# The last half pair in two quarters of queries, with four output blocks left behind the loop

## The chip, the cores and the metric

The kernel runs on one core of a Trainium2 chip. The metric is the device time of one execution in microseconds. Engines in this text: TensorE (PE, its weight loads PEld), VectorE (DVE), ScalarE (ACT), GpSimd (POOL) and SyncE (SP), which here only issues DMAs.

## The reference

```python
# x: 2048 rows (S) of 512 (D); 32 heads of 16
g = sigmoid((x * gate_w).sum(-1, keepdims=True))
q, k, v = heads of x @ wqkv
a = (softmax(q @ k.T / 4) @ v, heads side by side) @ wo
b = Re(DFT over the rows of the DFT over the columns of x)   # as products with four given matrices
return g * a + (1 - g) * b
```

All arrays are float32. The softmax runs over all 2048 keys for each of the 2048 queries and 32 heads.

## The kernel before

Rows come in 16 blocks of 128 (`NB`), heads in 16 pairs (`NP`). Large products run in the format float32r with each operand split into a rounded part and a rest; three products of the parts (rounded x rounded, rounded x rest, rest x rounded) make one full product. `halves_of` (L201) issues such a product as two 64-row matmuls that run side by side on the array, one into each bank of a two-bank PSUM tile. One call of it is a "pair" in this text.

The main loop (L1217) has 512 steps: 16 pairs of heads, for each two halves of 1024 queries (h), for each 16 blocks of keys (kb). A step computes the scores of two heads, 128 keys and 1024 queries (`qk`, two times 512 queries, c = 0 and 1: the first into the two-bank tile "wide1", the second into single banks), their exponentials on ScalarE, and the values (`pv`): four matmuls, for c and the head j, each into 17 rows (16 of values, one of sums) of one PSUM bank `pvb`, summed over the 16 key blocks. Values are taken two steps at a time, in even steps, one or two steps behind the scores. After a half, `quotients` copies pvb to SBUF and gathers the sums, and `divide` some steps later divides and stores the rows in DRAM, from where they are loaded again as operands.

Step numbers: pair p begins at step 32 p. From step 285 (MIX) on, each step takes one piece of other TensorE work, the fill (`next(fill)`), from a generator `outputs`. In an even step the fill stands ahead of that step's scores, in an odd step behind them. So the queue of TensorE reads: odd step's scores, odd step's fill, even step's fill, even step's scores, values of two steps, next odd step's scores.

From step 461 on the fill is the output projection. `mix_heads(t, steps)` makes output block t from the first 12 pairs of heads in nine pairs of matmuls, spread over as many steps as `steps` has numbers, (4, 5) being four pairs in the first step and five in the second, and (2, 2, 2, 3) for blocks 0, 2 and 4. `mix_some(t, (0, 1))` adds pairs 12 to 15 of the heads to the blocks t and t + 4: part 0 and part 1, three pairs each; for t of 8 to 11 there is a part 2, which is the last half pair (pair 15, second 1024 queries). Each of these takes its two banks from `pair_banks()`, the tile "wide0" of a pool with one buffer, and ends with `take_in`, two instructions on VectorE that read the two banks, weigh them with g and add them to the rows y. `store_out` sends finished rows out on SP's queue.

The fill at the end of the loop is: blocks 0 to 15 by `mix_heads` (steps 461 to 498), `mix_some` for 8, 9, 10, then 0, 1, 2 (499 to 510), one empty piece. Behind the loop (from L1284) the last half pair's values are copied, turned by TensorE so that the sums lie beside them, divided, turned back and rounded; then come the parts that are left: block 3's (with 7), all of 11's (with 15), and part 2 of 8, 9, 10 and 11 (with 12 to 15).

Of the kernel before, what the change touches and what calls it, by code (L numbers as in the profile page):

```python
# [52 lines left out]
HALVED = MIX + NB * (LATER - CROSS)  # L53
SLOW = 3
EVERY = 24
# [13 lines left out]
def build(tc, xT, xr, wqkv, wo, wrT, wiT, cr, ci, ct, gate, out):  # L69
    nc = tc.nc  # L70
    with ExitStack() as ctx:
# [152 lines left out]
        def qk(p, h, kb, c, pss):  # L224
# [3 lines left out]
            for j in range(2):  # L228
                b = 64 * j
                nc.tensor.matmul(pss[j], ks[b:b + 50, kb * P:(kb + 1) * P],  # L230
                                 qs[b:b + 50, q0:q0 + 512], start=True, stop=True)

        psk, order_ = [], ["d0", "d1", "k0"]

# [538 lines left out]
        with ExitStack() as pa:  # L773
# [21 lines left out]

            def pv(p, h, kb, es):
                for c, j, r in quads:
                    nc.tensor.matmul(pvb[r:r + VC, :], va[:, kb, 2 * p + j, :], es[c][j],  # L798
                                     start=kb == 0, stop=kb == NB - 1, tile_position=(0, r))

# [13 lines left out]
            def divide(p, h, ob, lc):  # L814
# [19 lines left out]
                store(1, ol)  # L834


            ys, oc = {}, {}
# [314 lines left out]

            def mix_some(t, parts):

                ps = pair_banks()
                ps = ps[:, 0, :], ps[:, 1, :]
                for k in parts:
                    mix_rest(t, ps, k, k == parts[0], k == parts[-1])
                    if k == parts[0]:
                        yield  # L1160
# [4 lines left out]
                yield  # L1165

            def outputs():

                for t in range(NB - LATER, NB - CROSS):
                    yield from spectral(t)  # L1170
                yield from crosses()
                for c in range(NC):
                    for t in range(4 * c, 4 * c + 4):
                        yield from mix_heads(t, (2, 2, 2, 3) if t < 2 * SLOW and t % 2 == 0 else (4, 5))
                    if c < 2:
                        output_rows(c + 2)
                for t in (8, 9, 10):
                    yield from mix_some(t, (0, 1))
                for t in range(3):
                    yield from mix_some(t, (0, 1))  # L1180
                yield

            groups = {}

            def part(t, *ks):

                if t not in groups:
                    if t in (3, 9):
                        ps = pair_banks()
                        groups[t] = ps[:, 0, :], ps[:, 1, :]  # L1190
                    else:
                        groups[t] = bank2() if t == 8 else (bank(), pvb if t == 11 else bank())
                for k in ks:
                    mix_rest(t, groups[t], k, k == 0 or 7 < t < 11, k == (2 if t > 3 else 1))

            now = [0]
            fill, operands = outputs(), output_operands()
            halves, halved, pend = [], [], []

# [17 lines left out]
            for step in range(NP * PERIODS):  # L1217
# [42 lines left out]
                if done and done[2] == NB - 1:  # L1260
                    halved.append((step + (10 if done[0] < NP - 2 else 7 if done[0] < NP - 1 else 3), quotients(*done[:2])))
                if halved and halved[0][0] <= step:
# [4 lines left out]
                    if p_ == NP - 2 + (h_ == 0):  # L1267
                        output_last(h_)
                pend.append((p, h, kb, es))
                sum_quarters(step)  # L1270
# [9 lines left out]

            halves_ = [slice(0, 256), slice(256, 512)]
            blocks_ = [slice(s * P, (s + 1) * P) for s in range(4)]
            ob = ap.tile([P, 512], F32, tag="ob", name="ob", bufs=2)
            oh, ol = (cw.tile([P, 512], F32R, tag=tag, name=tag) for tag in ("chi", "clo"))  # L1284
            direct[1].append((oh, ol))
            for c, copy in zip(halves_, (nc.vector.tensor_copy, nc.scalar.copy)):
                copy(ob[:, c], pvb[:, c])
            part(3, 1)
            turned, spread = bank(), bank()
            for q in blocks_:  # L1290
                nc.tensor.transpose(turned[:, q], ob[:, q], ident)  # L1291
            rl = sm.tile([P, 16], F32, tag="lc", name="lc")
            nc.vector.reciprocal(rl.rearrange("p (s n) -> p s n", n=4),
                                 turned.rearrange("p (s n m) -> p s n m", n=4, m=32)[:, :, :, DH])
            for i, c in enumerate(halves_):
                heads = [v.rearrange("p (n m) -> p n m", m=32) for v in (rb[:, c], turned[:, c])]
                nc.vector.tensor_mul(heads[0], heads[1],  # L1297
                                     rl[:, 8 * i:8 * i + 8].rearrange("p (n m) -> p n m", m=1).to_broadcast([P, 8, 32]))
            for q in blocks_:
                nc.tensor.transpose(spread[:, q], rb[:, q], ident)  # L1300
            part(11, 0, 1)

            def scaled(t, j):

                o = ap.tile([P, D], F32, tag="take", name="take", bufs=3)
                nc.scalar.mul(o, groups[t][j], g[:, t + 4 * j:t + 4 * j + 1])
                nc.gpsimd.tensor_add(ys[t + 4 * j], ys[t + 4 * j], o)

            scaled(3, 0)
            for c in halves_:  # L1310
                nc.scalar.copy(oh[:, c], spread[:, c])
            for c in halves_:
                nc.vector.tensor_sub(ol[:, c], spread[:, c], oh[:, c].bitcast(F32))
            scaled(3, 1)
            store_out(3)
            for t in (8, 9, 10, 11):
                part(t, 2)
            for j in range(2):
                scaled(9, j)
            for t in (8, 10, 11):  # L1320
                for j in range(2):
                    take_in(t + 4 * j, groups[t][j])
            for j, queue in enumerate((nc.sync, nc.scalar)):
                for t in (8, 10, 9, 11):
                    queue.dma_start(out[(t + 4 * j) * P:(t + 4 * j + 1) * P, :], ys[t + 4 * j])

# [26 lines left out]
```

## Time and profile before

| what | value |
|---|---|
| three runs | 1700.26, 1700.48, 1703.22 us, median 1700.48 |
| the profiled execution | 1700.53 us, span 1698.7 us |
| granted TensorE clock | 0.999 |
| matmuls busy (TensorE) | 99% of the span |
| ScalarE busy | 90% |
| VectorE busy | 68% |
| GpSimd busy | 46% |

The span runs from the first to the last instruction of the profiled execution. [...] In the chain of waits each piece is the work that the next piece had to wait for. In a line of the timeline, what stands in brackets is the time in which the engine was idle ahead of the instruction and what ended it.

### The profile page before, as it was taken

The page shows a single profiled execution, that of the slowest core. Times are in us where ns is not written, and L with a number is a line of the kernel's source. Part 1 is how long each engine was busy: PE and PEld are TensorE (multiplying, and loading weights), DVE is VectorE, ACT ScalarE, POOL GpSimd, SP SyncE. Part 2 cuts the span into 40 slices and gives each one's busy share as a digit, 9 for nine tenths or more (in the row PEclk, how much of TensorE's full clock was granted, in tenths as well). Part 3 has the DMA queues.
Part 4 walks back from the last instruction along what each step waited for, and adds up shares of the span by engine and source line. Part 5 has one row for each costly group of instructions (what it writes and reads, how often), then busy time and mean ns, then how long its engine had stood idle before and what let it go on. Part 6 is the DMA issues. An engine that isn't in the chain of part 4 may idle for free.

```text
span 1698.7 us, 34689 instructions
## 1 busy us (share of the span) xinstructions
PE 1684.6 (99%) x13524; PEld 1039.9 (61%) x13524; DVE 1147.9 (68%) x1563; ACT 1527.5 (90%) x2545; POOL 774.5 (46%) x958
## 2 busy tenths in 40 slices
PE   9999999999999999999999999999999999999998
PEld 7798999899899783343333333334555555555554
DVE  6689889899999986666666666666113456554343
ACT  6698889888888889999999999999888888888876
POOL 5446476655554842453453445444223333434222
PEclk9999999999999999999999999999999999999999
DMA  8793566544446665645544444534416456576833
GB/s 310 266 311 77 164 196 194 157 132 126 132 125 181 188 114 108 182 109 125 149 117 120 114 122 115 118 103 104 93 55 145 149 142 147 142 175 151 197 91 127
DMA packets 150516, 249.51 MB, mean 147 GB/s; under 512 B 49696, under 2 KB 60432, under 8 KB 142992
## 3 DMA queue, kind: packets, MB, share of 16 engines
q1 hardware_dynamic: 135088, 225.92, 49.3%
q0 software_dynamic: 14688, 20.33, 5.1%
q8 instruction: 106, 1.74, 0.5%
q10 hardware_dynamic: 576, 1.05, 0.2%
q14 instruction: 58, 0.48, 0.1%
HBM read 165.94 MB, written 81.01 MB: 145 GB/s over the span
## 4 chain that ended last, share of the span: by engine, by line
PE 65%; DVE 1%; issue 0%; DVEq 0%; ACT 0%
PE pvb L798 29%; PE s L230 19%; PE s L205 10%; PE s L155 4%; PE xy L205 2%; PE s L176 1%; DVE y L913 0%; DVE mx L181 0%; DVE c L404 0%; DVE b L318 0%; PE s L1300 0%; DVEq L1349 0%; PE s L1291 0%; ACT s L179 0%; DVE rb L1297 0%
## 5 line engine op out<-in xcount | busy, mean ns | idle before, releaser
L254 ACT ACTIVATE eb<-s 128x1024 f32<-128x1024 f32 x512 | 576.9, 1127 | 65.3 <-PE s L230 65.2
L262 ACT ACTIVATE e<-s 128x512 f32<-128x512 f32 x1022 | 607.4, 706 | 0.0
L181 DVE TENSOR_REDUCE mx<-s 128x1 f32<-128x512 f32 x740 | 490.9, 688 | 48.7 <-PE s L176 38.0
L798 PE MATMUL pvb<-eb,va 128*17 128x512 f32 x2052 | 511.5, 597 | 0.0
L798 PE MATMUL pvb<-e,va 128*17 128x512 f32 x2044 | 510.7, 597 | 0.0
L179 ACT ACTIVATE s<-s 128x512 f32<-128x512 f32 x740 | 424.1, 586 | 71.9 <-PE s L176 44.4
L157 DVE TENSOR_REDUCE mx<-s 128x2 f32<-128x1024 f32 x284 | 348.1, 1226 | 172.3 <-PE s L155 172.2
L230 PEld LDWEIGHTS s<-qs,ks 50*128 50x128 f32 x2048 | 214.0, 184 | 349.6 <-ACT eb L254 242.4
L230 PE MATMUL s<-qs,ks 50*128 50x512 f32 x2048 | 417.2, 434 | 0.0
L205 PE MATMUL xy<-b,c 64*128 64x512 f32 x2280 | 377.9, 391 | 1.3 <-POOL b L374 1.3
L176 PE MATMUL s<-ks,qs 64*128 64x512 f32 x1480 | 369.3, 397 | 3.2 <-issue 1.7
L205 PEld LDWEIGHTS xy<-b,c 64*128 64x128 f32 x2280 | 276.5, 184 | 20.4 <-POOL b L374 2.0
L176 PEld LDWEIGHTS s<-ks,qs 64*128 64x128 f32 x1480 | 203.3, 184 | 35.0 <-DVE mx L181 7.7
L798 PEld LDWEIGHTS pvb<-eb,va 128*17 128x17 f32 x2052 | 71.3, 96 | 192.0 <-issue 183.3
L817 POOL DMA_DIRECT2D r_d<-lc x31 | 18.0, 580 | 267.6 <-DVE lc L816 219.4
L205 PE MATMUL s<-b,b 64*128 64x512 f32 x1050 | 136.1, 390 | 0.0
L205 PE MATMUL xy<-w,b 64*128 64x512 f32 x768 | 120.2, 391 | 0.0
L810 POOL DMA_DIRECT2D lc<-ob x124 | 63.1, 516 | 124.3 <-DVE ob L807 114.1
L155 PE MATMUL s<-ks,qs 48*128 48x512 f32 x568 | 114.7, 394 | 0.0
L205 PEld LDWEIGHTS s<-b,b 64*128 64x128 f32 x1050 | 99.5, 185 | 23.9 <-issue 1.0
L819 POOL DMA_DIRECT2D rb<-r_d x124 | 60.5, 495 | 99.0 <-DMA r_d<-lc 96.1
L405 POOL TENSOR_TENSOR c<-craw,c 128x512 fp32r<-128x512 f32 x76 | 98.2, 1292 | 14.8 <-DVE c L404 6.2
(143 smaller groups left out, 1571.1 us busy)
## 6 DMA issues: line engine op xcount, KB each, us to landing
qs<-q_d SPq DMA_DIRECT2D x92, 256.0 KB
craw<-cr SPq DMA_DIRECT2D x60, 256.0 KB
ks<-kf_d SPq DMA_DIRECT2D x48, 256.0 KB
craw<-ct SPq DMA_DIRECT2D x48, 256.0 KB
ks<-k_d SPq DMA_DIRECT2D x44, 256.0 KB
kept_None<-sum SPq DMA_DIRECT2D x40, 256.0 KB
craw<-kept_None SPq DMA_DIRECT2D x40, 256.0 KB
craw<-ci SPq DMA_DIRECT2D x32, 256.0 KB
```

The costliest lines, as they stand in the source:

```text
L155: nc.tensor.matmul(ps[:, j, :], qs[b:b + 48, qb * P:(qb + 1) * P], ks[b:b + 48, c * 512:(c + 1) * 512], start=True, stop=True)
L157: nc.vector.tensor_reduce(mx[p][:, :, qb, c], ps, axis=AX.X, op=ALU.max)
L176: nc.tensor.matmul(ps, qs[b:b + 64, qb * P:(qb + 1) * P], ks[b:b + 64, c * 512:(c + 1) * 512], start=first, stop=True, skip_group_check=True)
L179: nc.scalar.activation(ps, ps, AF.Relu)
L181: nc.vector.tensor_reduce(mx[p][:, j, qb, c // 2:c // 2 + 1], ps, axis=AX.X, op=ALU.max)
L205: nc.tensor.matmul(ps[j], lhs[r], rhs[r], start=first, stop=last)
L230: nc.tensor.matmul(pss[j], ks[b:b + 50, kb * P:(kb + 1) * P], qs[b:b + 50, q0:q0 + 512], start=True, stop=True)
L254: nc.scalar.activation(e, ps, AF.Exp, scale=SCALE)
L262: nc.scalar.activation(e[j], pss[j], AF.Exp, scale=SCALE)
L405: sub(lo, raw, hi.bitcast(F32))
L798: nc.tensor.matmul(pvb[r:r + VC, :], va[:, kb, 2 * p + j, :], es[c][j], start=kb == 0, stop=kb == NB - 1, tile_position=(0, r))
L810: nc.gpsimd.dma_start(lc[32 * n:32 * n + 32, :], ob[r + DH:r + VC, :].rearrange("p (s e) -> p s e", e=16))
```

## The change

For the second half of pair 15 only, a step takes two key blocks of one quarter (512 queries) where it took one key block of both. After eight steps the first quarter is summed over all keys; its two halves of the sum lie in different rows of pvb and are added on VectorE (`quarter_sums` at step 504, `quarter_divided` two steps on, `quarter_rounded` four steps on, with the transfers on SP's queue). Part 2 of blocks 8 and 9 then is made from it by `mix_quarter` in the last piece of fill, and that of 10 and 11 right behind the loop. Part 0 and 1 of 11 and 15 come into the fill, in three steps. `SLOW` is now a table: block 0 in four steps, block 2 in three, all others in two. Behind the loop the second quarter is handled with a small matrix `pairs` (the identity's two halves of columns added), which adds the two halves of the sum while it turns them, and block 3 with 7 is made there whole.

```diff
-SLOW = 3
+SLOW = {0: (2, 2, 2, 3), 2: (3, 3, 3)}
...
+        def keys_at(p, h, kb):
+            if (p, h) == (NP - 1, 1):
+                return [(2 * (kb % 8) + n, kb // 8) for n in range(2)]
+            return [(kb, 0), (kb, 1)]
...
-            qk(p, h, kb, 0, [ps[:, j, :] for j in range(2)])
+            qk(p, h, *keys_at(p, h, kb)[0], [ps[:, j, :] for j in range(2)])
...
-            qk(p, h, kb, 1, pss)
+            qk(p, h, *keys_at(p, h, kb)[1], pss)
...
             def pv(p, h, kb, es):
+                half = (p, h) == (NP - 1, 1)
                 for c, j, r in quads:
-                    nc.tensor.matmul(pvb[r:r + VC, :], va[:, kb, 2 * p + j, :], es[c][j],
-                                     start=kb == 0, stop=kb == NB - 1, tile_position=(0, r))
+                    nc.tensor.matmul(pvb[r:r + VC, :], va[:, keys_at(p, h, kb)[c][0], 2 * p + j, :], es[c][j],
+                                     start=kb == 0 or half and kb == 8, stop=kb == NB - 1 or half and kb == 7,
+                                     tile_position=(0, r))
...
+            def mix_quarter(ps, halves_of_it, s):
+                for n, (a, b) in enumerate(((0, 0), (0, 1), (1, 0))):
+                    for j in range(2):
...
+                        nc.tensor.matmul(ps[j], tile_[r, at:at + P], w4[2][b][r], start=n == 0, stop=n == 2)
+
+            def quarter_sums():
+                ob = ap.tile([P, 512], F32, tag="ob", name="ob", bufs=2)
+                nc.vector.tensor_copy(ob, pvb)
+                lq = sm.tile([64, 2, 16], F32, tag="lc", name="lq")
+                for c, j, r in quads:
+                    nc.sync.dma_start(lq[32 * j:32 * j + 32, c, :],
+                                      ob[r + DH:r + VC, :].rearrange("p (s e) -> p s e", e=16))
+                os = ap.tile([P, 512], F32, tag="take", name="os", bufs=3)
+                for c in range(2):
+                    nc.sync.dma_start(os[64 * c:64 * c + 64, :], ob[64 - 64 * c:128 - 64 * c, :])
+                return ob, lq, os
+
+            def quarter_divided(ob, lq, os):
+                nc.vector.tensor_add(lq[:, 0, :], lq[:, 0, :], lq[:, 1, :])
+                nc.vector.reciprocal(lq[:, 0, :], lq[:, 0, :])
+                r_q = r_d[NP - 1][1][0:2, :]
+                nc.sync.dma_start(r_q.rearrange("n (s e) -> (n s) e", e=16), lq[:, 0, :])
+                for c, j, r in quads:
+                    nc.sync.dma_start(rb[r:r + DH, :], r_q[j:j + 1, :].to_broadcast([DH, 512]))
+                nc.vector.tensor_add(ob, ob, os)
+
+            def quarter_rounded(ob, lq, os):
+                nc.vector.tensor_mul(ob, ob, rb)
...
+                nc.vector.tensor_copy(oh, ob)
+                nc.vector.tensor_sub(ol, ob, oh.bitcast(F32))
...
-                        yield from mix_heads(t, (2, 2, 2, 3) if t < 2 * SLOW and t % 2 == 0 else (4, 5))
+                        yield from mix_heads(t, SLOW.get(t, (4, 5)))
...
                 for t in (8, 9, 10):
                     yield from mix_some(t, (0, 1))
+                yield from mix_some(11, (0, 1), (2, 2, 2))
                 for t in range(3):
                     yield from mix_some(t, (0, 1))
+                ps = pair_banks()
...
+                mix_quarter(ps, first_quarter, 0)
+                for j in range(2):
+                    take_in(8 + j, ps[j])
+                    nc.sync.dma_start(out[(8 + j) * P:(9 + j) * P, :], ys[8 + j])
                 yield
...
-                if step == NP * PERIODS - 1:
-                    part(3, 0)
...
+            mix_quarter(c8, first_quarter, 2)
             turned, spread = bank(), bank()
-            for q in blocks_:
-                nc.tensor.transpose(turned[:, q], ob[:, q], ident)
+            for s in range(4):
+                nc.tensor.matmul(turned[:, 64 * s:64 * s + 64], obs[s // 2][:, (s % 2) * P:(s % 2 + 1) * P], pairs,
+                                 start=True, stop=True)
...
-            for q in blocks_:
-                nc.tensor.transpose(spread[:, q], rb[:, q], ident)
-            part(11, 0, 1)
+            t3 = bank2()
+            mix_rest(3, t3, 0, True, False)
+            for s in range(4):
+                for r in (0, 64):
+                    nc.tensor.matmul(spread[r:r + 64, s * P:(s + 1) * P], sq[s // 2][:, 64 * (s % 2):64 * (s % 2) + 64],
+                                     ident, start=True, stop=True, tile_position=(0, r))
+            mix_rest(3, t3, 1, False, True)
+            for j in range(2):
+                scaled(10 + j, c8[j])
...
-            for t in (8, 9, 10, 11):
-                part(t, 2)
+            ends = [(bank(), pvb), pair_banks()]
...
+            for i in range(2):
+                mix_quarter(ends[i], last, 2 * i)
+            for j in range(2):
+                scaled(3 + 4 * j, t3[j])
+                send(3 + 4 * j, nc.sync)
+            for n in range(4):
+                take_in(12 + n, ends[n // 2][n % 2])
+                send(12 + n, nc.scalar)
```

How the instructions stand now, by the order of the built programs; in brackets is what an instruction waits for. TensorE before, from the end of output block 13 (tile s_21551) to the begin of block 14 (s_21602); L230 are scores, L798 values:

```order
L205 MATMUL s_21551<-b_20375,b_21256 128x512 x2
L205 MATMUL s_21551<-b_20374,b_21258 128x512 x2
L230 MATMUL s_21573<-qs,ks 128x512 [waits Activation_49]
...
L798 MATMUL pvb<-e_2_9906,va 17x512
...
L230 MATMUL s_21592<-qs,ks 128x512 [waits Activation_49]
...
L205 MATMUL s_21602<-b_20366,b_21248 128x512 [waits DVE_49]
L205 MATMUL s_21602<-b_20367,b_21248 128x512 x2
```

The same place of the changed program, block 13 being s_21494 and block 14 s_21545:

```order
L205 MATMUL s_21494<-b_20376,b_21186 128x512 x2
L205 MATMUL s_21494<-b_20377,b_21186 128x512 x2
L205 MATMUL s_21494<-b_20376,b_21188 128x512 x2
L205 MATMUL s_21545<-b_20368,b_21178 128x512 [waits DVE_49]
L205 MATMUL s_21545<-b_20368,b_21178 128x512
L205 MATMUL s_21545<-b_20369,b_21178 128x512 x2
L205 MATMUL s_21545<-b_20368,b_21180 128x512 x2
L205 MATMUL s_21545<-b_20372,b_21182 128x512 x2
L230 MATMUL s_21554<-qs,ks 128x512 [waits Activation_49]
```

Scores and values no longer stand between the two blocks: block 14 begins behind the last pair of block 13, in the same tile, and its first matmul waits for VectorE. It stands so at the begin of blocks 3 to 15 and of the four `mix_some` that follow; from `mix_some(0)` on the blocks are apart again.

TensorE behind the loop before, up to the first matmul of part 2 (chi and clo are the last half pair, rounded and rest):

```order
L1291 MATMUL s_22018<-ident,ob 128x128 [waits DVE_49]
...
L1300 MATMUL s_22019<-ident,rb 128x128 [waits DVE_49]
...
L205 MATMUL s_22032<-b_20738,b_21396 128x512
L205 MATMUL pvb<-b_20738,b_21396 128x512
L205 MATMUL s_22057<-b_20743,chi 128x512 [waits Activation_49]
```

and in the changed program, from the last values on (oh and ol are the first quarter):

```order
L805 MATMUL pvb<-e_2_9909,va 17x512
L1193 MATMUL s_22055<-b_20745,oh 128x512 [waits DVE_49]
...
L1356 MATMUL s_22062<-pairs,ob 128x64 [waits DVE_49,Pool_49]
...
L205 MATMUL s_22074<-b_20735,b_20944 128x512 [waits PE_49]
...
L1370 MATMUL s_22063<-ident,sq 64x128 [waits DVE_49]
...
L205 MATMUL s_22074<-b_20740,b_21754 128x512 x2
...
L1193 MATMUL s_22111<-b_20745,chi 128x512 [waits Activation_49]
```

There the six pairs for blocks 11 and 15 and the twelve pairs of part 2 have become three pairs from the first quarter, six for blocks 3 and 7 and six from the second quarter.

VectorE at the end of the loop before, with the take-ins of the last two blocks and the copy behind the loop:

```order
L913 SCALAR_TENSOR_TENSOR y_19939<-s_21902,g,y_19939 128x512 [waits PE_49]
L913 SCALAR_TENSOR_TENSOR y_20052<-s_21902,g,y_20052 128x512
L913 SCALAR_TENSOR_TENSOR y_19939<-s_21947,g,y_19939 128x512 [waits PE_49]
L913 SCALAR_TENSOR_TENSOR y_20052<-s_21947,g,y_20052 128x512
L1287 COPY ob<-pvb 128x256 [waits PE_49,Pool_49]
```

and in the changed program:

```order
L1198 COPY ob<-pvb 128x512 [waits PE_49,Pool_49]
L924 SCALAR_TENSOR_TENSOR y_19941<-s_21884,g,y_19941 128x512 [waits PE_49]
L1210 TENSOR_TENSOR lq<-lq 64x16 [waits DMAHW5_49,DMAHW4_49,DMAHW6_49,DMAHW3_49,DMASW5_49]
L1216 TENSOR_TENSOR ob<-ob,os 128x512 [waits DMAHW7_49,DMAHW0_49]
L924 SCALAR_TENSOR_TENSOR y_19941<-s_21937,g,y_19941 128x512 [waits PE_49]
L1220 TENSOR_TENSOR ob<-ob,rb 128x512 [waits DMAHW6_49,DMAHW5_49,DMAHW7_49,DMAHW4_49,DVE_49]
L1222 CAST oh<-ob 128x512 [waits DMASW2_49,DMASW3_49,DVE_49,Pool_49]
L1223 TENSOR_TENSOR ol<-ob,oh 128x512 [waits DMASW5_49,DMASW4_49,DVE_49]
L924 SCALAR_TENSOR_TENSOR y_19941<-s_21987,g,y_19941 128x512 [waits PE_49]
```

The first quarter's waits for transfers now stand between the take-ins of blocks 0, 1 and 2 (with 4, 5 and 6).

More of the change, by code (lines that the diff above doesn't have):

```diff
@@ L1268, in build @@
                         output_last(h_)
+                for n, make in ((2, quarter_divided), (4, quarter_rounded)):
+                    if ended and step == ended[0][0] + n:
+                        make(*ended[0][1])
                 pend.append((p, h, kb, es))
@@ L1314, in build, with scaled @@
-            scaled(3, 1)
-            store_out(3)
-            for t in (8, 9, 10, 11):
-                part(t, 2)
-            for j in range(2):
[L1319 to L1325, printed above, removed]
+            def scaled(t, ps):
+                o = ap.tile([P, D], F32, tag="take", name="take", bufs=3)
+                nc.scalar.mul(o, ps, g[:, t:t + 1])
+                nc.gpsimd.tensor_add(ys[t], ys[t], o)
@@ new lines, in send @@
+            def send(t, queue):
+                queue.dma_start(out[t * P:(t + 1) * P, :], ys[t])
+            halves_ = [slice(0, 256), slice(256, 512)]
+            obs = [ap.tile([P, 512], F32, tag="ob", name="ob", bufs=2)[:, 0:256] for i in range(2)]
+            for o, c, copy in zip(obs, halves_, (nc.vector.tensor_copy, nc.scalar.copy)):
+                copy(o, pvb[:, c])
+            c8 = pair_banks()
+            c8 = c8[:, 0, :], c8[:, 1, :]
+            mix_quarter(c8, first_quarter, 2)
```

76 lines of the change are left out of this document (38 added, 38 removed).

## The prediction

> **What bounds the kernel now.** I read the page first, then the chain of waits in order of time for the stretch that the change touches (steps 461 to 511 and what stands behind the loop), then the timeline of TensorE and VectorE there, and last the tail in windows.
>
> ```profile
> core 0: 1698.7 us, clock 0.999
> PE 1684.6 (99%) x13524; PEld 1039.9 (61%) x13524; DVE 1147.9 (68%) x1563; ACT 1527.5 (90%) x2545; POOL 774.5 (46%) x958
> ```
>
> TensorE is busy all the time, so what counts is how much the change adds to its queue, and where it makes it wait. ScalarE, at 90%, is close behind. The chain (start, length, engine, tile, line, instructions) shows the steps:
>
> ```profile
> 1562.77 0.93 PE s L205 x8
> 1567.15 1.15 PE s L205 x10
> ...
> 1644.48 2.07 PE s L205 x18
> 1646.55 0.47 PE s L230 x4
> 1647.03 1.84 PE pvb L798 x16
> 1648.87 0.66 PE s L230 x4
> 1649.52 2.07 PE s L205 x18
> ...
> 1654.56 1.39 PE s L205 x12
> 1658.94 1.38 PE s L205 x12
> ...
> 1667.68 1.88 PE s L205 x12
> ...
> 1681.28 0.69 PE s L205 x6
> ```
>
> L205 is the fill work, in pairs of 64-row matmuls (x18 is nine pairs). I call a group what runs from the fill of an odd step to that of the next odd step: the odd step's fill, the even step's, scores (0.47), two steps' values (1.84), scores (0.66). The 2.97 us beside the fill are the same in each. A pair takes 2.07 / 9 = 0.23. A group of nine pairs takes 1649.52 - 1644.48 = 5.04. One of six takes 1658.94 - 1654.56 = 4.38, and one of four takes 1567.15 - 1562.77 = 4.38 too: below six pairs the exponentials of ScalarE set the time, and pairs cost nothing. This adds up: before, the 25 groups from 1562.77 to 1681.28 have nine pairs 13 times and four to six 12 times, 13 x 5.04 + 12 x 4.375 = 118.0; the real stretch is 118.5, and the 0.5 is the one long piece at 1667.68 (1.88 where 1.39 is usual), a wait for rows of pair 15 from DRAM.
>
> **Part one: the phase of the blocks.** Before, every output block of the fill begins in an odd step and ends in an even one. Its pairs then stand together, and scores and values stand between it and the next block. The new numbers (3 steps for block 2, 2 for block 4) let blocks 3 to 15 and the next four (8 to 11 again) begin in an even step, directly behind the last pair of the block before, which is in the same place of the queue with nothing between. All blocks use the one two-bank tile "wide0", and the first matmul of each waits for VectorE, which must have read the tile. What that reading takes, and when it starts, is in the timeline:
>
> ```profile
> 1644.32 2.23 PE L205 MATMUL s<-b,b 64*128 64x512 f32 x18
> 1646.39 0.64 PE L230 MATMUL s<-qs,ks 50*128 50x512 f32 x4
> 1646.60 1.54 DVE L913 SCALAR_TENSOR_TENSOR y<-s,g,y 128x512 f32<-128x512 f32 x2 [2.84 <-PE s L205]
> 1649.36 2.23 PE L205 MATMUL s<-b,b 64*128 64x512 f32 x18
> 1656.02 1.41 DVE L913 SCALAR_TENSOR_TENSOR y<-s,g,y 128x512 f32<-128x512 f32 x2 [2.66 <-PE s L205]
> ```
>
> The block's last matmul ends at 1646.55, VectorE takes it in from 1646.60 to 1648.14, and TensorE comes back to the tile at 1649.36, so today this is hidden with 1.2 us to spare. Without scores and values between, TensorE would have gone on at 1646.39 and must now stand until after 1648.14. The way back from VectorE and the price of an empty pipeline are in the tail, where this does happen:
>
> ```profile
> 1686.06 0.43 DVE rb L1297
> 1686.49 0.04 issue
> 1686.54 0.77 PE s L1300 x4
> ```
> ```profile
> L205 PE MATMUL s<-b,b x1050: 383/390/502, 1317.9 to 1688.5; 64*128 64x512 f32 x175
> ```
>
> VectorE to TensorE takes 0.04; a matmul that follows an idle time takes 0.50 (the longest) and not 0.39 (the median), 0.11 more. So one wait costs 0.16 (1646.55 - 1646.39) + 0.05 + 1.54 + 0.04 + 0.11 = 1.9. It is 1.8 for the blocks taken in at 1.41 (two rows of y and not twice the same). The blocks that begin so are 3 to 15 (13), then 8, 9, 10 and 11 for pair 14's part (4), so 17 waits; 14 read a block of the first kind and three one of the second: 14 x 1.91 + 3 x 1.78 = 32.1. ScalarE can't hide it: the group gets longer between its odd and its even scores, where only groups under six pairs have room. One of the 17, at steps 501 and 502 with five pairs, hides 0.2. I take +31.8. From below the rows give 17 x 1.5 (the two reads alone), 25.5; from above, with 0.2 more for each restart, 36.
>
> Nothing else waits worse for it: ScalarE then idles, and every transfer for the later blocks (heads' rows, y, pair 14's rows) gets 1.9 us more for each block. Block 8's y is now taken in at step 481 and is asked for at 480, some 8 us earlier, so I cost that at nothing.
>
> **Part two: work moved into the loop.** The first two parts of blocks 11 and 15 come into the fill (six pairs); all six pairs of blocks 3 and 7 are now behind the loop, and the first quarter's three pairs for blocks 8 and 9 stand in step 511 in the place of three of them. The loop had 183 pairs and has 189. By groups: ten of six pairs or fewer, one of seven, one of eight, thirteen of nine: 10 x 4.375 + 4.59 + 4.82 + 13 x 5.04 = 118.7, against 118.0: +0.7. The wait of 0.5 at 1667.68 is for data that leave at step 496; between there and step 506 there now stand three or four waits of 1.8, so it goes: -0.5.
>
> Taking two key blocks of one quarter a step, and not one key block of two quarters, changes no count and no shape: same scores, exponentials and value matmuls. I cost it at nothing.
>
> **Part three: the first quarter's division.** It runs beside the loop from step 504: a copy on VectorE, six DMAs on SP's queue, an addition and a reciprocal, a store, four loads, four more VectorE instructions, and the result is wanted at step 511, about 14 us after the values of step 504 end. The same kind of chain for pair 15's first half, on POOL's queue, shows the hops, and two groups of other tiles the price on VectorE:
>
> ```profile
> 1649.98 1.97 POOL L810 DMA_DIRECT2D lc<-ob  x4 [14.79 <-DVE ob L807]
> 1653.65 0.57 POOL L817 DMA_DIRECT2D r_d<-lc  x1 [1.70 <-DVE lc L816]
> 1659.18 1.28 POOL L820 TENSOR_TENSOR ob<-ob,rb 128x512 f32<-128x512 f32 x1 [1.60 <-DMA rb<-r_d]
> ```
> ```profile
> L868 DVE TENSOR_TENSOR b<-wor,b 128x512 fp32r<-128x512 f32 x6 | 4.2, 693 | 0.2
> L867 DVE CAST b<-wor 128x512 fp32r<-128x512 f32 x6 | 2.5, 418 | 2.2 <-DMA yt_d<-turn 2.2
> ```
>
> Gather to store 3.7, store to product 5.5, with 1 us for the copy: about 10 to 11 us, then product, cast and difference on VectorE, 0.69 + 0.42 + 0.69 = 1.8: 12 to 13. It just fits; the cover is 1 us. VectorE waits in order here (its take-ins of blocks 1 and 2 stand behind these waits), and behind them TensorE, whose next block needs the tile. I take 0, and 1.5 from above if the hops are slower on SP's queue, where the stores of finished rows also stand.
>
> **Part four: behind the loop.**
>
> ```profile
> 1684.18 0.91 PE s L205 x6
> 1685.08 0.60 PE s L1291 x4
> 1685.71 0.27 DVE lc L1293
> 1689.62 2.76 DVE y L913 x4
> ```
> ```profile
> 1691.07 2.50 POOL L1307 TENSOR_TENSOR y<-y,take 128x512 f32<-128x512 f32 x2 [1.12 <-DVE y L913]
> 1690.40 3.00 SPq L1325 DMA_DIRECT2D out_dram<-y  x4
> ```
> ```profile
> L1306 ACT ACTIVATE take<-s,g 128x512 f32<-128x512 f32 x4 | 2.7, 690 | 1.7 <-PE s L205 1.7
> ```
> ```profile
> 1690.00:1691.00 1.00, 1.00 (x12) 0.81 (x10) 1.00 (x3) 0.70 (x2) 0.00 (x0) 1.00 0.20 74
> 1691.00:1692.00 1.00, 0.62 (x6) 0.19 (x2) 1.00 (x3) 0.57 (x1) 0.93 (x1) 1.00 1.01 375
> 1694.00:1695.00 1.00, 0.00 (x0) 0.00 (x0) 0.00 (x0) 0.00 (x0) 0.00 (x0) 1.00 1.02 371
> 1696.00:1697.00 1.00, 0.00 (x0) 0.00 (x0) 0.00 (x0) 0.00 (x0) 0.00 (x0) 0.50 1.01 373
> 1697.00:1698.00 1.00, 0.00 (x0) 0.00 (x0) 0.00 (x0) 0.00 (x0) 0.00 (x0) 0.50 0.04 12
> ```
>
> The last three columns are the granted clock, the DMA engines' share and GB/s: the DMA engines are full from about 1691 to 1697. Eight blocks of 0.262 MB become ready together, 0.69 us each at 380 GB/s, so the drain, not VectorE's last instruction, ends the run, 12.9 us after the last values (1684.18). After the change only six blocks (3, 7, 12 to 15) are late. From the last values: copies as before 0.9; the four 128x64 products 0.9; reciprocal 0.3; two products of 128x128 0.6, beside three pairs; eight 64x128 products 1.2, begun 0.2 before those end; three pairs 0.7 (the rounding lies beside them); two times three pairs, 0.7 each. The first two last blocks are complete at 5.3, VectorE takes four in from 5.4 to 8.2 at 0.69, ScalarE's two for block 3's tile at 0.69 and POOL's two at 1.25 behind them end at 7.9. The first is ready at 6.1; 0.5 to start, six times 0.69: 10.7, so -2.2. The prices of the float32 products aren't in the trace. From below they take no more than the transposes did, 0.60 + 0.77 = 1.37 for what I put at 2.1 (-2.9 in all); from above 24 instructions at a transpose's 0.19, 4.6 (+0.3). I stay nearer the transposes, as these have half the columns or half the rows.
>
> **The sum:** +31.8 + 0.7 - 0.5 + 0 - 2.2 = +29.8. On the profiled execution's own 1700.53, which is the median of the runs (1700.48) to 0.05, that gives 1730.3. The bounds give 25.3 + 0.7 - 0.5 - 2.9 = +22.6 and 36 + 0.7 + 1.5 + 0.3 = +38.5.
>
> **The rivals.** (1) The waits cost nothing, because the reading is over when TensorE gets there. Then the rest is left: 0.7 - 0.5 - 2.2 = -2.0, 1698.5. It would take a reading of under 0.2 us, or a second tile; for it speaks only that the same instructions stand in both queues' totals. It decides where a wait falls under 0.1 us; the change is faster by over 0.2% (3.4 us, about what a measurement of this kernel can tell from no change) only with the tail at its lower bound and more. I give this 0.06.
>
> (2) The idle times make the granted clock fall. Row first: after TensorE's last matmul, in the window 1691 to 1692, the clock stays 1.00 through 1694 to 1695 and is 0.50 in 1696 to 1697, so some 4 us of idleness are needed, and mine are 1.9. If it fell all the same, nine pairs would take 4.14 for 2.07 in each of 17 groups, +35 more: 1765. I give it 0.04.
>
> [...]
>
> (3) The first quarter comes late as well, by more than its bound, since VectorE, SP and TensorE wait for each other in order: over 1738. 0.04.
>
> **How the numbers follow.** The forecast has 0.86: 1730.3, range 1722 to 1738 from its bounds, rounded; it leaves out the three rivals, 1.4 in 10. Faster 0.02, same 0.05 (rival 1 for the most part), slower 0.93.
>
> **What would show it.** In the changed kernel, TensorE's matmuls at L205 should wait for VectorE's take-in (L924) 17 times, about 1.6 to 1.9 each, some 30 us in all, where before there is no such wait; groups of nine pairs should be 6.9 long and not 5.04; ScalarE should idle that much more; the clock should stay 0.99 or higher. The tail, from the last values to the end of the DMA traffic, should be 10 to 11.5 and not 12.9. Wrong would be: no waits at L205 (rival 1), a lower clock (rival 2), or TensorE waiting for oh or ol at L1193 (rival 3).

## The result and the profile after

The changed kernel takes 1730.1 us (median of five runs, 1727.25 to 1730.82) against 1700.48 before: a ratio of 1.0167, with a 95% interval of 1.0156 to 1.0178. The forecast was 1730.3. The profiled execution took 1730.1 us with a span of 1728.3, 29.6 above the span before. The total agrees to 0.2; several of its parts were off, and their errors nearly cancel.

In the changed kernel `take_in` is L924 (before L913), and the values are L805 (before L798). The page, engines' busy time:

```profile
PE 1687.3 (98%) x13540; PEld 1036.9 (60%) x13540; DVE 1150.9 (67%) x1572; ACT 1526.7 (88%) x2545; POOL 775.5 (45%) x959
```

TensorE is busy 2.7 us more, and the span is 29.6 longer: most of the new time is idle time of TensorE. What TensorE waited for from 1560 us on (total, times, longest), first before, then after:

```profile
PE s L1300 <- DVE rb L1297: 0.9, 1, 0.9
```
```profile
PE s L205 <- DVE y L924: 27.4, 17, 1.6
PE s L1193 <- DVE y L924: 1.0, 1, 1.0
```

Seventeen new waits for the take-in, and one more at L1193, the first quarter's part. Two groups in the chain of waits (start, length, what), and then a third in which something else happens:

```profile
1589.63 1.17 PE s L205 x10
...
1590.82 0.76 DVE y L924
...
1591.61 0.76 DVE y L924
...
1592.41 1.19 PE s L205 x8
1593.61 0.46 PE s L230 x4
1594.07 1.84 PE pvb L805 x16
1595.91 0.67 PE s L230 x4
1596.58 1.17 PE s L205 x10
...
1607.98 3.50 PE pvb L805 x16
```

Five pairs end one block, VectorE reads its two banks one after the other, then the four pairs of the next block follow. The group takes 1596.58 - 1589.63 = 6.95 where it took 5.04: 1.91 more. In the third group the same sixteen value matmuls take 3.50 and not 1.84, although nothing is waited for. The windows (length, busy time of PE, PEld, DVE, ACT, POOL with instructions, then the granted clock, which the profile gives as a share of TensorE's full speed, the DMA share and GB/s) say why:

```profile
1607.90:1611.40 3.50, 3.50 (x18) 0.51 (x16) 0.00 (x0) 1.90 (x3) 0.00 (x0) 0.52 0.00 0
1683.00:1686.50 3.50, 3.50 (x18) 1.43 (x20) 0.00 (x0) 1.80 (x3) 1.86 (x4) 0.52 0.04 7
```

The clock was halved for 3.41 us (0.50 from 1683.11 to 1686.52), twice in the loop. Each costs 3.50 - 1.84 = 1.7 us.

The tail (the same windows' columns):

```profile
1722.00:1723.00 1.00, 0.00 (x0) 0.00 (x0) 1.00 (x3) 0.00 (x0) 1.00 (x2) 1.00 0.38 141
1723.00:1724.00 1.00, 0.00 (x0) 0.00 (x0) 0.69 (x2) 0.00 (x0) 0.76 (x1) 1.00 1.01 379
1726.00:1727.00 1.00, 0.00 (x0) 0.00 (x0) 0.00 (x0) 0.00 (x0) 0.00 (x0) 0.50 0.80 289
```

The last values end at 1715.5, the DMA traffic at about 1726.9: 11.4 us, and 12.9 before.

Where the 29.6 come from, by the starts of the same work in both traces. The first stage, up to the first scores at L230, is 5.2 *shorter* (first L230 at 628.8 and 634.0, rows below), with the same instructions. The loop from the first group of step 461 to step 511's fill takes 154.7 (1558.0 to 1712.7) where it took 118.5: +36.2. The tail gives back 1.5. Together +29.5; what lies between these points, 0.4 more ahead of step 461 and 0.3 less at the end, nearly cancels.

### The profile page after: what moved, and what is told of

It reads as the page before. It is cut to its first block, busy times and chain, and to the rows that moved or that the text cites. A ratio compares the mean times of both kernels' runs of the same rounds, so it can differ in the third digit from the quotient of the medians.

```text
span 1728.3 us, 34744 instructions
## 1 busy us (share of the span) xinstructions
PE 1687.3 (98%) x13540; PEld 1036.9 (60%) x13540; DVE 1150.9 (67%) x1572; ACT 1526.7 (88%) x2545; POOL 775.5 (45%) x959
## 4 chain that ended last, share of the span: by engine, by line
PE 62%; issue 2%; DVE 1%; POOL 0%; DMA 0%; ACT 0%; POOLq 0%; DVEq 0%
PE pvb L805 28%; PE s L230 18%; PE s L205 9%; PE s L155 4%; PE xy L205 2%; DVE y L924 1%; PE s L176 1%; POOL y L1342 0%; DMA rb<-r_d 0%; DMA r_d<-lc 0%; DMA lc<-ob 0%; POOL rb L827 0%; DVE b L324 0%; POOL lc L818 0%; DVE mx L181 0%
## 5 line engine op out<-in xcount | busy, mean ns | idle before, releaser
L260 ACT ACTIVATE eb<-s 128x1024 f32<-128x1024 f32 x512 | 574.1, 1121 | 100.5 <-PE s L230 100.5
L805 PE MATMUL pvb<-eb,va 128*17 128x512 f32 x2052 | 513.9, 599 | 0.0
L805 PE MATMUL pvb<-e,va 128*17 128x512 f32 x2044 | 512.9, 599 | 0.0
L230 PEld LDWEIGHTS s<-qs,ks 50*128 50x128 f32 x2048 | 213.0, 185 | 349.5 <-ACT eb L260 241.7
L230 PE MATMUL s<-qs,ks 50*128 50x512 f32 x2048 | 416.8, 434 | 0.0
L205 PE MATMUL xy<-b,c 64*128 64x512 f32 x2280 | 375.3, 389 | 1.4 <-POOL b L380 1.4
L176 PE MATMUL s<-ks,qs 64*128 64x512 f32 x1480 | 367.0, 396 | 1.9 <-DVE mx L181 1.3
L205 PEld LDWEIGHTS xy<-b,c 64*128 64x128 f32 x2280 | 280.6, 184 | 14.8 <-POOL b L380 2.0
L176 PEld LDWEIGHTS s<-ks,qs 64*128 64x128 f32 x1480 | 204.3, 184 | 34.5 <-DVE mx L181 8.1
L805 PEld LDWEIGHTS pvb<-eb,va 128*17 128x17 f32 x2052 | 71.4, 96 | 195.1 <-issue 186.9
L205 PE MATMUL s<-b,b 64*128 64x512 f32 x1056 | 140.8, 395 | 27.4 <-DVE y L924 27.4
L205 PEld LDWEIGHTS s<-b,b 64*128 64x128 f32 x1056 | 98.1, 185 | 56.3 <-DVE y L924 34.7
L205 PE MATMUL xy<-w,b 64*128 64x512 f32 x768 | 118.9, 388 | 0.0
L411 POOL TENSOR_TENSOR c<-craw,c 128x512 fp32r<-128x512 f32 x76 | 98.1, 1290 | 14.8 <-DVE c L410 6.2
```

Of the source, the lines that this page charges most:

```text
L176: nc.tensor.matmul(ps, qs[b:b + 64, qb * P:(qb + 1) * P], ks[b:b + 64, c * 512:(c + 1) * 512], start=first, stop=True, skip_group_check=True)
L205: nc.tensor.matmul(ps[j], lhs[r], rhs[r], start=first, stop=last)
L411: sub(lo, raw, hi.bitcast(F32))
L805: nc.tensor.matmul(pvb[r:r + VC, :], va[:, keys_at(p, h, kb)[c][0], 2 * p + j, :], es[c][j], start=kb == 0 or half and kb == 8, stop=kb == ...
```

## The experiments

**1. The blocks begin in an odd step again.** The change, with block 2 in four steps and the first two parts of 11 and 15 in two. All else of the change stays.

```diff
-SLOW = {0: (2, 2, 2, 3), 2: (3, 3, 3)}
+SLOW = {0: (2, 2, 2, 3), 2: (2, 2, 2, 3)}
...
-                yield from mix_some(11, (0, 1), (2, 2, 2))
+                yield from mix_some(11, (0, 1))
```

> All of the change but its phase: block 2 in four steps again and blocks 11 and 15 in two, so that every block of the fill begins in an odd step. Theory (17 waits of TensorE for VectorE's take-in cost 1.9 each): the 17 waits are gone, TensorE waits for the take-in at most once (at the first quarter's matmuls, 1 us), the loop from step 461 to 511 takes 118 to 120 us and not 154.7, and the time is 1696 to 1701. Rival A (the quarter's transfers and divisions on VectorE and SP are what costs): it stays near 1730. Rival B (the granted clock falls after idle times, and this is most of the loss): the clock is back at 0.999, as in the theory, but the waits alone would have cost under 15.

Measured: 1696.33 us, ratio to the kernel before 0.9968 (0.9957 to 0.9979). The list of the matmuls' waits is empty from 1550 us on, the loop takes 119.9 (1558.8 to 1678.7), and the clock doesn't fall in it. One loss is not in that list: the matmuls for block 0 (with 4) take 2.88 where the others of six pairs take 1.55, 1.3 more. The kernel before loses 0.5 at the same place (2.05), where its weight loads wait 0.35 for the rows of pair 15 from DRAM (`b<-o_d`, to 1668.75); I put the 1.3 of number 1 down to the same rows.

```profile
1659.88 1.55 PE L205 MATMUL s<-b,b 64*128 64x512 f32 x12
1664.25 2.88 PE L205 MATMUL s<-b,b 64*128 64x512 f32 x12
```

So the order of the blocks alone carries the loss, 33.8 us of it by the medians. The loop's difference is 34.8: two falls of the clock 3.4, the wait at L1193 1.0, and 31.7 for the 17 waits, 1.9 each, less the 1.3 for the rows of pair 15, which number 1 pays and the change doesn't. The first stage is 1.0 longer in number 1 (first scores at 629.9). That it also beats the kernel before is more than the tail explains; numbers 8 to 12 are about that.

**2. The first quarter's rounding two steps later.** On top of number 1:

```diff
-                for n, make in ((2, quarter_divided), (4, quarter_rounded)):
+                for n, make in ((2, quarter_divided), (6, quarter_rounded)):
```

> As the run with all blocks in the odd phase, and the first quarter is divided and rounded at step 510, behind the take-in of blocks 2 and 6, not at step 508 ahead of it. Theory: the 1.0 that TensorE waits at the first quarter's matmuls (for the take-in that stands behind the rounding) goes, so 1.0 less than the run with the odd phase alone: 1695 to 1700, and not slower than before. Rival: the rounding then comes too late itself, and TensorE waits as long for oh or ol.

Measured: 1696.38 us, 0.9971 (0.9960 to 0.9983), no different from number 1. There was nothing to gain, since number 1 has no wait at L1193 either. It has none because TensorE, held up 1.3 us by the rows of pair 15, comes there 14.8 us behind the copy that begins the first quarter's chain (1663.89 to 1678.70); in the change it came 13.7 behind it and had to wait 1.0. In number 2 the rows cost 1.7, of which 0.5 stand in the list as a wait.

**3. The other way round: the kernel before, with blocks in even steps.** Block 2 in three steps, and 14 and 15 so that the last ones fit; nothing else of the change.

```diff
-                        yield from mix_heads(t, (2, 2, 2, 3) if t < 2 * SLOW and t % 2 == 0 else (4, 5))
+                        yield from mix_heads(t, {0: (2, 2, 2, 3), 2: (3, 3, 3), 14: (3, 3, 3), 15: (2, 2, 2, 3)}.get(t, (4, 5)))
```

> The kernel before with the phase alone: block 2 in three steps, blocks 3 to 13 in two, 14 in three, 15 in four, so that blocks 3 to 14 begin in an even step directly behind the block before; nothing of the quarters. Theory: 12 waits of 1.9, less 0.7 for work that goes to groups with room: +22, 1722 to 1726 with one or two falls of the clock at 1.7. Rival A (the quarters' work costs the time): same as before, 1700.

Measured: 1724.75 us, 1.0141 (1.0127 to 1.0155).

```profile
PE s L205 <- DVE y L913: 19.6, 12, 1.6
```

Twelve waits of 1.63, as in the change. At 1.91 a wait that is 22.9; with 1.7 for a fall of the clock, 24.6, and the difference of the medians is 24.3. The profiled execution had a fall at 1602, in the loop, and one at 63, in the first stage.

**4. Six waits and not seventeen.** As number 1, but block 8 in three steps, so that only blocks between 3 and 8 begin in an even step.

```diff
-SLOW = {0: (2, 2, 2, 3), 2: (3, 3, 3)}
+SLOW = {0: (2, 2, 2, 3), 2: (3, 3, 3), 8: (3, 3, 3)}
...
-                yield from mix_some(11, (0, 1), (2, 2, 2))
+                yield from mix_some(11, (0, 1))
```

> The change with only 6 blocks in the even phase (3 to 8; block 8 takes three steps and turns the phase back; 11 and 15 in two steps). Theory (each wait costs the same): 6 x 1.9 = 11.5, less 0.7, over the run with the odd phase: 1707 to 1712. Rival B (falls of the clock are most of it, and need many idle times close together): under 5 over that run.

Measured: 1709.59 us, 1.0044 (1.0030 to 1.0057), 13.3 above number 1.

```profile
PE s L205 <- DVE y L924: 9.8, 6, 1.6
```

Six times 1.91 and one fall of the clock are 13.2. Less 0.7 for pairs that come into groups with room, as was expected, and with 0.4 more for the rows of pair 15, that is the 12.9 by which the loop is longer than number 1's. The cost goes with the number of waits.

**5 and 6. Other work between two blocks.** The change, with its order of blocks; from step 469 on the even step's fill stands behind that step's scores (number 5), or behind its scores and values (number 6). So 0.47, or 2.3 us, of other matmuls stand between the last pair of a block and the first of the next.

```diff
-                if step >= MIX and step % 2 == 0:
+                if MIX <= step < OUT + 8 and step % 2 == 0:
...
-                if step >= MIX and step % 2:
+                if step >= MIX and (step % 2 or step >= OUT + 8):
```

> The change, but from step 469 on the even step's fill stands behind that step's scores and not ahead of them, so scores (0.47) lie between the 17 blocks and those before. Theory (the wait is the time from the block's last matmul to the end of VectorE's reading, less what stands between): each of the 17 groups 0.45 shorter, 6.5 for nine pairs and not 6.95, in all -7.7: 1720 to 1724. Rival (TensorE loses a fixed time by the change of tile or by the order, whatever stands between): 1727 to 1731, as the change.

Measured: 1720.62 us, 1.0124 (1.0110 to 1.0137).

```profile
PE s L205 <- DVE y L924: 13.6, 17, 0.9
PE s L230 <- ACT eb L260: 1.7, 8, 0.4
```
```profile
1611.28 1.18 PE s L205 x10
...
1612.49 0.76 DVE y L924
...
1613.28 0.76 DVE y L924
...
1614.08 1.19 PE s L205 x8
...
1617.78 1.18 PE s L205 x10
```

Still seventeen waits, each about half as long. The group takes 6.50, 1.46 above 5.04 and 0.45 below the change's 6.95, as was expected. The seventeen groups are together 24.2 longer than without waits. The four behind them are 2.5 longer although they have no wait, and the 1.3 for the rows of pair 15 is gone: the loop is 25.5 longer than number 1's in the profiled execution, and the median is 24.3 above. Here the clock did not fall in the loop.

Number 6:

```diff
-                if step >= MIX and step % 2 == 0:
+                if MIX <= step < OUT + 8 and step % 2 == 0:
...
+                if step >= OUT + 8 and step % 2 == 0:
+                    next(fill)
```

> The change in its even phase, but from step 469 on the even step's fill stands behind that step's scores and values. Theory: 2.31 of scores and values then cover the 1.9 of the reading and its way, so the 17 waits go, though the order of the blocks' steps is the change's own; an odd step's scores then stand only 1.8 ahead of the even step's, less than ScalarE's 2.07, which costs 0.25 a group: 1697 to 1704. Rival: the even phase costs by something else than the wait for the reading, and it stays over 1715.

Measured: 1707.12 us, 1.0040 (1.0024 to 1.0055); less was expected.

```profile
PE s L205 <- DVE y L924: 3.1, 3, 1.1
PE s L230 <- ACT eb L260: 1.2, 5, 0.4
PE s L1193 <- DVE y L924: 1.0, 1, 1.0
```
```profile
1613.77 1.15 PE s L205 x10
1614.92 0.71 PE s L230 x4
1615.63 1.84 PE pvb L805 x16
1617.47 1.12 PE s L205 x8
1618.60 0.47 PE s L230 x4
1619.07 1.15 PE s L205 x10
```

All seventeen waits are gone, by 2.3 us of other matmuls in the gap. The three in the list, and the one at L1193, are new and lie elsewhere: blocks 0, 1 and 2 and the first quarter begin in an odd step, and in this order only that step's scores stand ahead of them.

```profile
1671.51 0.96 PE L205 MATMUL s<-b,b 64*128 64x512 f32 x6 [1.04 <-DVE y L924]
```

The expectation had 0.25 a group for the order itself, and the groups take 5.30, 0.27 above number 1's 5.03: fill in two pieces takes 1.15 + 1.12 where one piece takes 2.07. What it lacked are the four new waits, 4.1 in all, and 0.5 to 0.8 in each of five smaller groups.

**7. A longer read.** The change, with one more reading of the first bank on VectorE ahead of `take_in`, its result unused, for all blocks from 2 on.

```diff
+                if t > 1:
+                    nc.vector.tensor_reduce(z[:, 0:1], ps[:, 0, :], axis=AX.X, op=ALU.max)
                 for j in range(2):
                     take_in(t, ps[:, j, :])
```

> The change, and VectorE reads the first bank of the tile of blocks 2 to 15 once more (a reduction of 128x512, 0.69) ahead of the take-in. It serves nothing in the output. Theory: 14 of the 17 waits are 0.69 longer, 2.6 and not 1.9, +9.7: 1737 to 1742 with the clock as it was. Rival B (falls of the granted clock grow with the idle time): more than two falls to 0.5 in the profile, and over 1743.

Measured: 1747.17 us, 1.0273 (1.0257 to 1.0289), 17.1 above the change.

```profile
PE s L205 <- DVE y L924: 35.8, 17, 2.2
```
```profile
1611.18 0.69 DVE z L1151
1611.88 0.67 DVE y L924
...
1612.57 0.76 DVE y L924
...
1615.07 3.44 PE pvb L805 x16
```

The waits grow by 8.4 in all, 0.6 for each of the fourteen, a little under the length of the added instruction (0.69). The expectation had 1737 to 1742 with the clock as in the change; but the clock fell five times in the loop here (one is the 3.44 above), three times more than in the change, 5 us; the granted clock of the whole execution is 0.993, and 0.997 in the change. The first stage was 2.5 longer, with a fall in it: its longest matmul of L176 takes 625 ns, and 502 in the change. The 1.3 for the rows of pair 15 is there, and the 1.0 at L1193 isn't. Together that is 16.2, and the profiled executions differ by 16.3.

**8 to 12. The first stage: where tiles lie.** The first 630 us hold the same instructions in both kernels, yet took 5.2 us less after, and number 1, without waits, beats the kernel before. One thing that the change does reach back there: its tile `lq` shares the tag "lc" with the 16 columns that `quotients` gathers, and has 32 columns, so the tiles allocated behind the tag's two buffers in SBUF move by 128 bytes. Number 8 is the kernel before with only that; 10, 11 and 12 have 24, 48 and 64 columns in the place of 32 (64, 256 and 384 bytes).

```diff
-                lc = sm.tile([P, 16], F32, tag="lc", name="lc")
+                lc = sm.tile([P, 32], F32, tag="lc", name="lc")[:, 0:16]
```

> The kernel before, and nothing of the change but the size of one small tile: lc gets 32 columns and not 16 (only 16 are used), as large as the change's lq makes it. This moves every SBUF tile that is laid out behind it by 128 bytes. Question: the first scores of the main loop begin at 629 to 630 in the three kernels made from the change that begin like it and at 634 to 637 in the two with the small tile, with the same instructions up to there. Theory (the places of the tiles make the first stage 4 to 6 faster): first scores at 628 to 631 and 1695 to 1697. Rival (it is something else of the change, or the chip's mood): 634 and 1700 to 1701.

Number 9 is the other way round: number 1, with `lq` as two tiles of 16 columns, so that the tiles lie as before.

```diff
-                lq = sm.tile([64, 2, 16], F32, tag="lc", name="lq")
+                lq = [sm.tile([64, 16], F32, tag="lc", name="lq") for c in range(2)]
...
```

> The change in the odd phase, with lq as two tiles of 16 columns, so that all SBUF tiles lie where they lay before. Theory of the places: first scores at 634 to 637, and 1699.5 to 1702, which is the kernel before less about 1 (loop +0.8, tail -1.5 to -2). Rival: 1696, as the run with the odd phase.

> The kernel before with lc of 24 columns, so the tiles behind it move by 64 bytes, half of what 32 columns do. If any move away from the old places is enough: 1695.5 to 1697, first scores at 629 to 630. If the gain goes with the distance: 1698 to 1699. If it takes 128 bytes: 1700.5, first scores at 634.

> The kernel before with lc of 48 columns, so the tiles behind it move by 256 bytes, twice of what 32 columns do. If any move is enough, or what counts comes from 128 bytes on: 1695.5 to 1697, first scores at 629 to 630. If places 256 bytes apart are alike: 1700.5, first scores at 634.

> The kernel before with lc of 64 columns: the tiles behind it move by 384 bytes, which is 128 more than 256. So far 128 bytes made the first stage 5 faster (first scores at 629 against 634) and 64 and 256 bytes did not. If places repeat every 256 bytes: first scores at 628 to 630 and 1695.5 to 1697. If 128 bytes is one place by itself: 633 to 635 and 1700 to 1702.

| kernel | moved by | time, us | ratio to before (95%) | first scores at |
|---|---|---|---|---|
| before | 0 | 1700.48 | 1 | 634.0 |
| 9, the change without waits, old places | 0 | 1700.51 | 1.0004 (0.9995 to 1.0013) | 633.5 |
| 10 | 64 bytes | 1701.87 | 1.0008 (0.9999 to 1.0017) | 634.5 |
| 8 | 128 bytes | 1696.12 | 0.9977 (0.9968 to 0.9986) | 628.8 |
| 11 | 256 bytes | 1700.28 | 0.9999 (0.9990 to 1.0007) | 632.9 |
| 12 | 384 bytes | 1695.39 | 0.9966 (0.9954 to 0.9978) | 631.0, with a fall of the clock |

Each ratio is to runs of the kernel before on the same chip, so it differs a little from the quotient of the times in this table.

The matmuls by line (count, shortest/median/longest in ns, first and last start), of before, 8 and 9; L176 is a line of the first stage, and L230's first start is its end:

```profile
L230 PE MATMUL s<-qs,ks x2048: 383/398/521, 634.0 to 1680.9; 50*128 50x512 f32 x187
L176 PE MATMUL s<-ks,qs x1480: 383/390/502, 57.0 to 633.0; 64*128 64x512 f32 x185
```
```profile
L230 PE MATMUL s<-qs,ks x2048: 383/397/516, 628.8 to 1675.9; 50*128 50x512 f32 x187
L176 PE MATMUL s<-ks,qs x1480: 383/386/503, 57.3 to 627.7; 64*128 64x512 f32 x185
```
```profile
L176 PE MATMUL s<-ks,qs x1480: 383/390/503, 56.8 to 632.5; 64*128 64x512 f32 x185
```

A place 128 or 384 bytes further makes the first stage some 4 to 5 us shorter, one 0, 64 or 256 bytes further doesn't. In the fast places (the change, 1, 8 and 12) the median matmul of L176 takes 386 ns, in before, 9 and 11 it takes 390, in 10 it takes 392. The 2280 matmuls of L205 into the tile xy, most of them in this stage, go the same way: 386 in the change, 8 and 12, and 389 in before, 9 and 11. So in the change the 5.2 us of the first stage come from the new tile's size, and not from what the tile is for. Numbers 1, 2, 8 and 12 beat both kernels. Number 12 has the lowest time, though its interval overlaps those of the other three; it is the kernel before with 48 unused columns in one small tile. Which tile's place it is, and why it counts, stays open. Number 9 also gives the price of all the rest of the change, without waits and in the old places: no difference that can be measured.

## Why the prediction came out right, point by point

- **The phase of the blocks, +31.8.** Right, in place, number and size. Seventeen waits of L205 for the take-in; a group of nine pairs takes 6.95, and 6.95 - 5.04 = 1.91 is the worked-out wait to the hundredth. The loop's +36.2, less 3.4 for the clock and 1.0 at L1193, leaves 31.8; the forecast had 31.8 + 0.7 - 0.5 = 32.0. Numbers 1 and 3 show the cause from both sides, 4 that it goes by number, 5 and 7 that what counts is the length of the read less what stands between, and 6 that 2.3 us between hide it.
- **ScalarE can't hide it.** Right: it idles ahead of `eb` 100.5 us in all in the change, and 66.9 in number 1.

```profile
L260 ACT ACTIVATE eb<-s 128x1024 f32<-128x1024 f32 x512 | 574.1, 1121 | 100.5 <-PE s L230 100.5
```
```profile
L260 ACT ACTIVATE eb<-s 128x1024 f32<-128x1024 f32 x512 | 574.3, 1122 | 66.9 <-PE s L230 66.8
```

- **Work moved into the loop, +0.7, and the wait for DRAM, -0.5.** The wait for the rows of pair 15 is gone in the change, as said, but the reason given for it, the waits of 1.8 ahead of it, isn't shown. Number 7 has these waits too, and its matmuls for block 0 still take 2.89 where 1.55 is usual. The waits hold up the data as well: in their chain VectorE takes a reciprocal 8.8 us behind the copy in the change (1673.90 to 1682.67), and 4.1 before (1649.00 to 1653.11). What the change has there and number 7 has not is a fall of the clock (at 1683): it holds TensorE back (that group takes 7.70, and 6.14 in number 7) and not the data (from the reciprocal to the product they take 6.1 in both). So the -0.5 may be luck. Without long waits the rows cost more than the 0.5 of before: 1.3 in numbers 1 and 9 (0.5 in number 8). Number 1's loop takes 119.9 against a worked-out 118.7, and these 1.3 are the difference; the +0.7 holds.
- **The first quarter's division, 0 (bound 1.5).** The cover was missed by 1.0. In the timeline of VectorE and TensorE:

```profile
1698.06 0.69 DVE L1198 COPY ob<-pvb 128x512 f32<-128x512 f32 x1 [1.46 <-PE pvb L805]
1709.36 0.69 DVE L1220 TENSOR_TENSOR ob<-ob,rb 128x512 f32<-128x512 f32 x1 [2.98 <-DMA rb<-r_d]
1710.14 0.43 DVE L1222 CAST oh<-ob 128x512 fp32r<-128x512 f32 x1
1710.60 0.69 DVE L1223 TENSOR_TENSOR ol<-ob,oh 128x512 fp32r<-128x512 f32 x1
1711.21 1.40 DVE L924 SCALAR_TENSOR_TENSOR y<-s,g,y 128x512 f32<-128x512 f32 x2
1712.67 0.73 PE L1193 MATMUL s<-b,oh 64*128 64x512 f32 x4 [0.96 <-DVE y L924]
```

  The chain itself took 11.3 to the product and 13.2 to `ol`, near the 10 to 11 and 12 to 13 that were said. But TensorE didn't wait for `ol`: it waited for the take-in of blocks 2 and 6, which stood behind `ol` on VectorE and holds the two-bank tile. The text had named that way of waiting, and put it at 0.
- **The tail, -2.2.** It was -1.5. The products with `pairs` took 1.10 (said 0.9), the turning back 1.09 (said 1.2), and VectorE's last four take-ins ran from 5.5 to 8.2 behind the last values (said 5.4 to 8.2). What was mis-sized is the start of the drain: by the windows above it is full only from about 1722.6, 7.1 behind the last values, and not from 6.6. The rest is the drain itself, 4.3 and not 4.1.

```profile
1716.29 1.10 PE L1356 MATMUL s<-pairs,ob 128*128 128x64 f32 x8
1718.22 1.09 PE L1370 MATMUL s<-ident,sq 128*64 128x128 f32 x16
```

- **Rival 2, the clock.** The argument against it failed. It said that some 4 us of idle time in one piece are needed, from a row where TensorE had stopped for good. Two halvings of 3.4 us came behind idle times of 1.6 and 1.5 (those at 1604.70 and 1681.31). The row itself was one sample of many: behind TensorE's last matmul the clock falls after 4.1 us before, 2.5 in the change and 2.1 in number 9. The cost stayed small, 3.4 us and not 35, because only two of seventeen waits brought a fall.
- **Not in the sum at all:** the 5.2 us that the first stage loses. It had the same instructions, and the forecast took its time as given.

- **Two slips in the sums.** 32.1 less 0.2 is 31.9 and not 31.8, and the bounds +22.6 and +38.5 give 1723 to 1739, where the range was put at 1722 to 1738. Neither changes a reading.

So the main term is shown right. That the total came within 0.2 us owes something to chance: 3.4 + 1.0 + 0.7 of missed costs against 5.2 of missed gain.

## What to carry to other kernels

Where two pieces of work share one PSUM tile, look at what stands in the matmul queue between the last matmul of the one and the first of the next: the time of the read, less that, plus the restart, was the price in these runs (1.9 us a group with nothing between, 1.46 with 0.47 us of other matmuls, and 2.3 us of them removed all seventeen waits). Look at every block that the new order touches: number 6 brought four waits to other blocks. A change that only counts steps can shift such a phase for all that follows it, so lay out the new order in full before costing anything. And before a difference of half a per cent is put down to an edit, time the kernel before with the edit's tile sizes alone.

## What the runs showed of the hardware

- **The granted clock fell to half behind some short idle times of TensorE, and not behind others as long.** With idle times of 1.5 to 1.64 us in the change, most of them 6.95 us apart, it fell behind two of 17 in the profiled execution; with 2.2 us (14 of the 17 in number 7) five times; with 0.8 (number 5) not at all in the loop. The two falls of the change are 3.41 us long each (0.50 from 1608.02 and from 1683.11 on) and cost 1.7. The second came behind an idle time of 1.50, while twelve of the thirteen of 1.64 brought none, so the length of one idle time doesn't decide it alone. What else does, no run shows.
- **The places of the tiles in SBUF were worth 4 to 5 us of 630**, with the same instructions: 128 and 384 bytes further is faster (the median matmul of the first stage takes 386 ns and not 390), 64 and 256 is not.
